# Fillers in two early slots of an attention kernel as rounds of four 32-row TensorE products

## The chip, the cores and the metric

The kernel runs on one core of one Trainium2 chip. The metric is the device time of one execution in microseconds. Before the change three executions took 212.06, 213.21 and 213.5 us; the median is 213.21 us. A fourth execution was profiled.

## The reference: what is computed

Block-sparse attention over 4 batches, 8 heads, 768 positions of 64 values, and then a gated feed-forward layer on its output:

```python
scores = scale * np.matmul(q, k.transpose(0, 1, 3, 2))
...            # mask: neighbouring blocks of 32, first and last block, 3 drawn blocks a row
attn = softmax(np.where(mask, scores, -1000000000.0))
x = (attn @ v) with the heads side by side              # (4, 768, 512)
h = np.maximum(x @ w_in, 0.0);  u, v = the two halves of h
v_n = (v - mean) / sqrt(var + 1e-06)
v_s = np.einsum('ts,bsd->btd', w_spatial, v_n) + b_spatial
out = (u * v_s) @ w_out
```

The mask goes into the scores as extra rows of the contraction: a head's K and Q have 64 rows of data and 24 rows for the blocks, 88 in all. The exponential needs no maximum, since the values are small, and the sum of a row comes from a column of ones next to V.

## The kernel before

All operations are written in one order by hand; each engine runs its own part of that order from the front, and waits on semaphores for what the others make. The middle of the program is a loop over *slots* (line 823). In a slot s the order is: the q·k products of that slot into a tile of two PSUM banks (`qk_unit`, L395 to L412, or `qk_full`, L414), whose exponential ACT then takes into `a_all` (L412, L424); products with V for an earlier slot (`av_unit`, L453, or `av_full`, L471); then whatever was put into the slot with `when`; then pieces of the feed-forward layer from a queue (`product`, L557).

The first slots are the start of the pipeline. Slots 0 to 2 are head 0, slots 3 to 5 head 1, each on two thirds of the queries; slots 6 to 8 are the first third of heads 2 and 3. K and Q arrive by DMA in float32, POOL casts them to bf16 (`nat`, L135), TensorE transposes them into PSUM, and DVE copies them from there into `kq` (L215). Slot 0 transposes the rest of head 0's K (`second`, PSUM tile `ps2`), slot 1 head 1's K and Q (`third`, tile `ps1`, five transposes, then four DVE copies), slot 4 the K and first Q of heads 2 and 3 (`tr_first`, L355). Products with V begin in slot 5, when the first V has been cast.

PSUM has eight banks here: two tiles of two banks each for the q·k products (tag `sc`), two banks with the tag `av`, and the banks `moeA` and `moeB`, which `moe_tag` hands out in turn. A tile whose bank was used before waits until its readers are done.

*Fillers* (L181 to L183) are products of a zero tile `warm` with itself, whose result nobody reads. There are 26 ahead of the first transposes, 6 and 2 among them, and 4 in slot 2 (`FILL3`, line 719). Those four multiply 128 rows by 128 columns into one bank, `moeA`.

Of the kernel before, what the change touches and what calls it, by code (L numbers as in the profile page):

```python
# [10 lines left out]
FP32 = mybir.dt.float32  # L11
# [15 lines left out]
def kernel(  # L27
# [16 lines left out]
    nc = tc.nc  # L44
# [21 lines left out]
    FILL, FILL2, FILL3 = 26, (6, 0, 2), 4  # L66
# [4 lines left out]
    psum = ctx.enter_context(tc.tile_pool(name="psum", bufs=1, space=bass.MemoryType.PSUM))  # L71
# [3 lines left out]
    warm = const.tile([128, 128], BF16)  # L75
# [103 lines left out]
    wps = psum.tile([128, 512], FP32, tag="av", bufs=2)  # L179

    def filler(n, to):  # L181
        for _ in range(n):
            nc.tensor.matmul(out=to[:, 0:128], lhsT=warm, rhs=warm, start=True, stop=True)  # L183

    filler(FILL, wps)

    def ts(out, in0, s1, o0, s2=None, o1=None):
        kw = {} if o1 is None else {"op1": o1}
        nc.vector.tensor_scalar(out=out, in0=in0, scalar1=s1, scalar2=s2, op0=o0, **kw)
# [68 lines left out]
    def moe_tag():  # L258
        moe_tags.rotate(1)
        if moe_tags[0] in held:  # L260
            moe_tags.rotate(1)
        return moe_tags[0]
# [446 lines left out]
    def when(slot, *fns):  # L709
        at.setdefault(slot, []).extend(fns)  # L710

    def c(f, *a, **kw):
        return lambda: f(*a, **kw)
# [2 lines left out]
    ROWS = [(1, 2, 8, qcols(0)), (1, 3, 4, K_), (5, 4, 6, K_), (8, 6, 8, K_), (14, 4, 8, qcols(1, 2))]  # L716
    when(0, second)
    when(1, third)
    when(2, lambda: filler(FILL3, psum.tile([128, 512], FP32, tag=moe_tag(), bufs=1, name="wps")))
    for p, sl in ((1, 4), (2, 7), (3, 10)):  # L720
        when(sl, c(tr_first, p))
    for sl, h0, h1, cs in ROWS:
# [152 lines left out]
```

## Time and profile before

| | |
|---|---|
| profiled execution, time | 213.02 us |
| its span, first to last instruction | 211.1 us |
| time outside the span | 1.9 us |
| PE (matmul) busy | 204.4 us, 97% |
| ACT busy | 170.8 us, 81% |
| DVE busy | 127.2 us, 60% |
| POOL busy | 82.4 us, 39% |
| share of PE in the chain that ended last | 90% |
| granted TensorE clock, mean | 1.000 |

PE is TensorE's matmul side, PEld its weight loads. A matmul's duration in the trace contains its way through the array, so products that follow each other overlap: how fast a stream runs is read from the distance between starts. In the timeline, consecutive instructions of one kind are one row: start, length from the first start to the last end, engine, line, operation, tiles and shapes, count, and in brackets the idle time before it and what ended it. With n products in a row, (length − duration of one) / (n − 1) is the distance of their starts. Durations of one, from the groups by shape in the first 12 us: 0.27 us for 88 x 256, 0.38 for 88 x 512, 0.22 for a transpose of 128 x 128, 0.19 for 128 x 65.

### The profile page before, as it was taken

Reading aid. Unit: us, or ns where it says so; the run is one execution under the profiler, and the core shown is the slowest. Engines: PE = TensorE matmul, PEld = TensorE weight load, DVE = VectorE, ACT = ScalarE, POOL = GpSimd, SP = SyncE. Lnnn points to the kernel's source line nnn. Section 1 sums busy time; section 2 is a strip of 40 time slices with the busy share of each in tenths; the row PEclk is TensorE's granted clock in tenths of the full one; section 3 lists DMA queues with packets and bytes.
Section 4 is the critical chain, followed back from the end, with each engine's and each line's share of the span. In section 5 each row is a group of like instructions: output and inputs, shape, how many; then the busy total and the mean of one; then the engine's idle time right before and its main releaser. Section 6 shows DMA issues by size and latency. Waiting matters only on the chain.

```text
span 211.1 us, 5352 instructions
## 1 busy us (share of the span) xinstructions
PE 204.4 (97%) x2143; PEld 129.6 (61%) x2143; DVE 127.2 (60%) x287; ACT 170.8 (81%) x226; POOL 82.4 (39%) x179
## 2 busy tenths in 40 slices
PE   8799999999999999999999999999999999999992
PEld 6578877756666666665666655665566656544441
DVE  7589786979454533394974454285884433476551
ACT  6988999999999999979998888979989787266021
POOL 5789679877882606062552051151020000012000
PEclk9999999999999999999999999999999999999999
DMA  5999899999999979999981497696101225520265
GB/s 147 335 369 343 240 352 285 271 240 324 264 373 163 308 176 292 210 298 313 189 237 37 109 253 179 215 314 124 37 3 32 55 53 107 198 83 2 50 170 203
DMA packets 63868, 41.96 MB, mean 199 GB/s; under 512 B 45668, under 2 KB 58596, under 8 KB 63844
## 3 DMA queue, kind: packets, MB, share of 16 engines
q1 hardware_dynamic: 63412, 41.24, 74.6%
q10 hardware_dynamic: 432, 0.39, 0.6%
q8 instruction: 16, 0.26, 0.5%
q14 instruction: 8, 0.07, 0.1%
HBM read 24.38 MB, written 6.29 MB: 145 GB/s over the span
## 4 chain that ended last, share of the span: by engine, by line
PE 90%; DMA 3%; DVE 2%; SPq 1%; ACT 1%; POOL 0%; issue 0%; ACTq 0%
PE ps_moe L557 33%; PE ps L420 22%; PE ps_av L471 13%; PE ps_t L557 8%; PE ps L407 6%; PE ps_av L453 4%; PE ps_sc L557 3%; DMA st_v<-in_v_dram 3%; DVE kq L215 1%; SPq L107 1%; PE ps_av L268 1%; PE ps L268 0%; ACT osb L218 0%; DVE xn L436 0%; POOL vv L135 0%
## 5 line engine op out<-in xcount | busy, mean ns | idle before, releaser
L424 ACT ACTIVATE a_all<-ps 128x768 bf16<-128x768 f32 x144 | 113.9, 812 | 14.3 <-PE ps L420 6.4
L420 PE MATMUL ps<-kq 88*128 88x384 bf16 x288 | 70.5, 325 | 0.1
L471 PEld LDWEIGHTS <-a_all 128*128 128x128 bf16 x864 | 46.4, 97 | 20.0
L471 PE MATMUL ps_av<-vv,a_all 128*128 128x65 bf16 x864 | 51.2, 194 | 0.0
L420 PEld LDWEIGHTS <-kq 88*128 88x128 bf16 x288 | 27.9, 98 | 30.5 <-issue 0.9
L557 PE MATMUL ps_moe<-w_in_t,xt 128*128 128x512 bf16 x144 | 44.0, 378 | 0.0
L412 ACT ACTIVATE a_all<-ps 128x1024 bf16<-128x1024 f32 x36 | 35.0, 1025 | 2.0 <-PE ps L407 1.8
L135 POOL CAST nat<-st_k 128x256 bf16<-128x256 f32 (+3 forms) x37 | 16.9, 486 | 42.5 <-DMA st_k<-in_k_dram 42.3
L557 PE MATMUL ps_moe<-vn,w_spt 128*128 128x512 bf16 x108 | 32.7, 378 | 0.0
L435 DVE RECIPROCAL rc<-ps_av 128x6 f32<-128x6 f32 (+1 forms) x36 | 6.7, 186 | 30.7 <-PE ps_av L471 29.2
L594 POOL TENSOR_SCALAR std<-mv 128x3 f32<-128x3 f32 (+1 forms) x9 | 2.1, 238 | 57.1 <-DVE mv L591 43.1
L625 DVE SCALAR_TENSOR_TENSOR un<-ps_moe,b_col,un 128x512 bf16<-128x512 f32 x18 | 13.5, 749 | 16.8 <-PE ps_moe L557 16.2
L407 PE MATMUL ps<-kq 88*128 88x256 bf16 (+1 forms) x140 | 21.6, 275 | 0.9 <-ACT a_all L412 0.7
L557 PE MATMUL ps_moe<-w_out_t,gt 128*128 128x512 bf16 x72 | 21.5, 378 | 0.0
L557 PEld LDWEIGHTS <-xt 128*128 128x128 bf16 x192 | 15.3, 97 | 7.0 <-DVE xt L215 0.2
L436 DVE TENSOR_TENSOR xn<-ps_av,rc 128x384 bf16<-128x384 f32 (+1 forms) x36 | 18.5, 513 | 1.2
L135 POOL CAST vv<-st_v 128x256 bf16<-128x256 f32 (+1 forms) x36 | 17.2, 509 | 3.0 <-DMA st_v<-in_v_dram 2.9
L135 POOL CAST nat<-st_q 128x256 bf16<-128x256 f32 (+1 forms) x38 | 16.3, 458 | 2.6 <-DMA st_q<-in_q_dram 2.4
L590 DVE BATCH_NORM_STATS2 stats<-vn 128x6 f32<-128x512 bf16 x24 | 16.5, 687 | 1.4 <-ACT vn L585 0.9
L407 PEld LDWEIGHTS <-kq 88*128 88x128 bf16 x140 | 12.5, 97 | 4.7 <-issue 0.8
L453 PE MATMUL ps_av<-vv,a_all 128*128 128x65 bf16 x288 | 14.8, 194 | 0.3 <-POOL vv L135 0.3
L453 PEld LDWEIGHTS <-a_all 128*128 128x128 bf16 x288 | 13.7, 98 | 1.8 <-issue 0.6
(84 smaller groups left out, 207.2 us busy)
## 6 DMA issues: line engine op xcount, KB each, us to landing
st_v<-in_v_dram SPq DMA_DIRECT2D x16, 384.0 KB, 5.8
out_dram<-osb SPq DMA_DIRECT2D x23, 256.0 KB, 2.8
st_k<-in_k_dram SPq DMA_DIRECT2D x15, 384.0 KB, 4.6
st_q<-in_q_dram SPq DMA_DIRECT2D x15, 384.0 KB, 5.2
ws_f<-in_moe_w_spatial_dram SPq DMA_DIRECT2D x6, 384.0 KB, 6.4
w_f<-in_moe_w_in_dram SPq DMA_DIRECT2D x8, 256.0 KB, 5.9
w_f<-in_moe_w_out_dram SPq DMA_DIRECT2D x4, 256.0 KB, 4.2
st_q<-in_q_dram SPq DMA_DIRECT2D x2, 128.0 KB, 4.8
```

Source lines behind the costliest of these rows:

```text
L135: eng.tensor_copy(out=dst, in_=src)
L407: nc.tensor.matmul(out=ps[:, at:at + n * TW], lhsT=kq[:, h, ci * 128:(ci + 1) * 128], rhs=kq[:, h, qcols(t0, n)], start=True, stop=True)
L412: nc.scalar.activation(out=out, in_=ps, func=AF.Exp, scale=0.125)
L420: nc.tensor.matmul(out=ps[:, hf * 512:hf * 512 + HALF], lhsT=kq[:, j % H, ci * 128:(ci + 1) * 128], rhs=kq[:, j % H, S + hf * HALF:S + (hf ...
L424: nc.scalar.activation(out=a_ref["h", j][:, ci, :].rearrange("p (b c) -> p b c", b=2), in_=ps.rearrange("p (b c) -> p b c", b=2)[:, :, 0:H ...
L435: nc.vector.reciprocal(out=rc[:, 0:n], in_=ps[:, :, D:VA])
L436: nc.vector.tensor_tensor(out=out, in0=ps[:, :, 0:D], in1=rc[:, 0:n].to_broadcast([128, n, D]), op=ALU.mult)
L453: nc.tensor.matmul(out=av_ref[u][:, to, :], lhsT=a_ref[u][:, at:at + 128], rhs=vv[pp % NVV][:, h, ci, :], start=(ci == 0), stop=(ci == NCH ...
L471: nc.tensor.matmul(out=av_ref[j][:, qc, :], lhsT=a_ref["h", j][:, ci, qc * 128:(qc + 1) * 128], rhs=vv[p % NVV][:, h, ci, :], start=(ci == ...
L557: nc.tensor.matmul(out=ref["ps"][:, 0:w], lhsT=lhs(i), rhs=rhs(i), start=(i == 0), stop=(i == n - 1))
L590: nc.vector.bn_stats(out=stats, in_=self.vn[:, tcc, :])
L625: nc.vector.scalar_tensor_tensor(out=self.un[:, tcc, :], in0=ps, scalar=b_col[:, tcc:tcc + 1], in1=self.un[:, tcc, :], op0=ALU.add, op1=AL ...
```

## The change

The four fillers of slot 2 give way to a new helper, `tiled_filler`, and slot 3 gets one too. The helper takes four PSUM tiles, one in each of the banks `moeA`, `moeB` and the two `av` banks. It issues one product over all 128 rows with 256 columns, then three rounds of four products that each use 32 rows (rows 0 to 31, 32 to 63, 64 to 95, 96 to 127) and one of the four banks, and then one over all rows again. The products of 32 rows have 256 columns in slot 2 and 512 in slot 3. The moving operand reads the 128 columns of `warm` over and over. All that is 14 products where there were 4 in slot 2, and 14 where there were none in slot 3.

```diff
+    def tiled_filler(n):
+        tags = ("moeA", "moeB", "av", "av")
+        to = [psum.tile([128, 512], FP32, tag=x, bufs=2 if x == "av" else 1, name=f"wps{i}")
+              for i, x in enumerate(tags)]
+        rhs = warm.rearrange("p (o n) -> p o n", o=1)
+
+        def mm(i, rs, w):
+            nc.tensor.matmul(out=to[i][:, 0:w], lhsT=warm[rs],
+                             rhs=rhs[rs].to_broadcast([rs.stop - rs.start, w // 128, 128]),
+                             start=True, stop=True)
+
+        mm(0, slice(0, 128), 256)
+        for i in range(3):
+            for r in range(4):
+                mm(r, slice(32 * r, 32 * r + 32), n)
+        mm(0, slice(0, 128), 256)
...
-    when(2, lambda: filler(FILL3, psum.tile([128, 512], FP32, tag=moe_tag(), bufs=1, name="wps")))
+    when(2, c(tiled_filler, 256))
+    when(3, c(tiled_filler, 512))
```

In the built program only TensorE's list differs; DVE, ACT, POOL and SP have the same instructions, in the same order and with the same waits. Three waits on TensorE are new or moved. The second product of 32 rows in slot 2 writes `moeB`, which held `ps1`, so its weight load waits for the last of the four DVE copies of `ps1`. Before, the q·k products of slot 3 waited for the third of these copies and those of slot 4 for the fourth. The first product of slot 3's fillers and the first transpose of slot 4 wait for earlier products on TensorE itself. The call of `moe_tag` for the old fillers is gone, so from slot 4 on `moeA` and `moeB` change places.

## The prediction

> **What bounds the kernel.** I read the table of engines, the chain that ended last, and then the timeline of the first 20 us, where the change lies.
>
> ```profile
> PE 204.4 (97%) x2143; PEld 129.6 (61%) x2143; DVE 127.2 (60%) x287; ACT 170.8 (81%) x226; POOL 82.4 (39%) x179
> ...
> PEclk9999999999999999999999999999999999999999
> ...
> PE 90%; DMA 3%; DVE 2%; SPq 1%; ACT 1%; POOL 0%; issue 0%; ACTq 0%
> ```
>
> TensorE is the chain: 90% of the span. What is not TensorE lies at the start, where loads, casts and DVE copies lead (the chain in order of time has DVE pieces up to 18.05 us, and after that nearly nothing but PE). So the question is how much later TensorE enters its unbroken stretch.
>
> ```profile
> 6.85 1.36 DVE L215 COPY kq<-ps 64x384 bf16<-64x384 bf16 x4 [0.31 <-PE ps L281]
> ...
> 7.08 0.59 PE L407 MATMUL ps<-kq 88*128 88x512 bf16 x2 [0.27 <-ACT a_all L412]
> 7.51 0.39 PE L183 MATMUL wps<-warm 128*128 128x128 bf16 x4
> 8.09 0.60 PE L407 MATMUL ps<-kq 88*128 88x256 bf16 x4 [0.19 <-ACT a_all L412]
> 8.91 0.60 PE L407 MATMUL ps<-kq 88*128 88x256 bf16 x4 [0.23 <-ACT a_all L412]
> 9.35 0.50 PE L268 MATMUL ps<-ident,nat 128*128 128x128 bf16 x6
> 10.34 0.28 PE L268 MATMUL ps<-ident,nat 128*128 128x128 bf16 x2 [0.49 <-POOL nat L135]
> 10.46 0.60 PE L407 MATMUL ps<-kq 88*128 88x512 bf16 x2
> 11.40 0.41 PE L453 MATMUL ps_av<-vv,a_all 128*128 128x65 bf16 x8 [0.34 <-POOL vv L135]
> ...
> 13.24 0.18 DVE L435 RECIPROCAL rc<-ps_av 128x4 f32<-128x4 f32 x1 [0.45 <-PE ps_av L453]
> ...
> 18.10 0.61 PE L407 MATMUL ps<-kq 88*128 88x256 bf16 x4 [0.24 <-DVE kq L215]
> ```
>
> The rows at 7.08, 8.09, 8.91 and 10.46 are the q·k products of slots 2, 3, 4 and 5; the old fillers stand at 7.51, the place of the new ones is after 7.51 and after the row at 8.09. TensorE has idle time there (0.19 + 0.23 + 0.49 + 0.34 us in brackets), and the new fillers may use it. From 18.10 us on the trace has no idle time of TensorE over 0.1 us up to 190 us, so what arrives late there ends late.
>
> **Prices.** Distances of starts, from the rows above: 0.11 us for 256 columns ((0.60 − 0.27)/3), 0.21 for 512 columns, 0.057 for 128 columns, 0.031 for 65 columns ((0.41 − 0.19)/7), which is as fast as the trace shows a weight load with its product to follow another. One product of the trace uses 24 rows (a mask product, between two that use the whole array):
>
> ```profile
> 4.83 0.48 PE L274 MATMUL mq<-kq,bm 88*128 88x256 bf16 x2
> 5.04 0.28 PE L274 MATMUL mq<-kq,bm 24*128 24x256 bf16 x1
> 5.25 0.29 PE L183 MATMUL wps<-warm 128*128 128x128 bf16 x2
> ```
>
> The first of these rows holds the 88-row product at 4.83 and the 24-row one. Each step takes 0.21 us where 256 columns take 0.11: changing over costs 0.10 us, in and again out.
>
> What the trace does not show is four 32-row products beside each other. Per product the bounds are 0.031 us (each starts as soon as its pair can be issued) and 0.11 or 0.21 us (columns one after another), or even 0.21 and 0.31 if each is charged the step of the 24-row row. I take the first: a round's products have their own rows, weights and banks, the program gives none of them a wait on another, and the trace starts independent pairs 0.031 us apart. A round then lasts the longer of 4 × 0.031 = 0.12 and its columns: 0.12 us in slot 2, 0.21 in slot 3. [...]
>
> **The sum, part by part.** Removed: four fillers, 4 × 0.057 = 0.23 us. They stood before an idle time and gain nothing.
>
> Slot 2: full product at 7.51, change-over, first 32-row product at 7.72. The second waits for the fourth DVE copy, which ends at 6.85 + 1.36 = 8.21; a release takes about 0.05 us (the cast of V ends at 11.35, its product starts at 11.40) and a weight load 0.03, so 8.30. Behind this wait stands all of TensorE's list. Then ten more steps of 0.031, 0.11 for the last one's columns, 0.10 to change over, 0.11 for the last full product: slot 3's q·k at 8.93 instead of 8.09, 0.84 late. ACT, which had run without a pause, now waits for it.
>
> Slot 3: 4 × 0.11, then 0.11 + 0.10 to the first 32-row product at 9.58; three rounds to 10.30; 0.10 and 0.11: slot 4's q·k at 10.51 instead of 8.91, 1.60 late.
>
> Slot 4 and 5: the eight transposes now follow at once (the cast they waited for ends at 10.29), which wins back 0.66: slot 5's q·k at 11.40 instead of 10.46, 0.94 late. The exponential of slot 4 starts at 11.15 (fourth product at 10.84, duration 0.27, release 0.04) and that of slot 5 at 12.07, since ACT starts one each 0.92 us; before, 11.09. It ends at 13.09. The DVE copies of the transposes move from 10.66 to 11.61.
>
> Slots 6 and 7: slot 6's q·k needs the first of these copies (12.29) and starts at 12.35, 0.70 late. Slot 7's q·k needs slot 5's PSUM tile, so ACT's end at 13.09: it starts at 13.14 instead of 12.35, 0.79 late. The V products after it release the reciprocal that stood at 13.24, so it comes at 14.03; its 0.45 us of idle time are already used up by the same delay. From the reciprocal on DVE works without a pause until the copy that TensorE awaits at 18.10. So TensorE's unbroken stretch starts 0.8 us later, and so does the end.
>
> 213.02 + 0.8 = **213.8 us** for an execution like the profiled one, which lies 0.2 below the median of the runs shown. POOL and the loads do not wait for this work, and their times stay; the swap of `moeA` and `moeB` I cost at nothing, since both are used alike in turn. Free change-overs would bring 213.4, change-overs of twice the size 214.2.
>
> **Rivals.**
> *The rounds run one after another.* For: the only small-row product of the trace overlaps with nothing. Columns in series make slot 2's fillers 11 × 0.11 after the wait and slot 3's 12 × 0.21: slot 3 at 9.72, slot 4 at 13.1 (4.2 late), slot 5 3.5 late, slot 7 3.4 late, end 216.4. If only the weight loads come one after another (about 0.10 us each by their rows), slot 4 is 2.9 late and the end 215.1. With the 24-row step for every product slot 4 is 6.3 late and the end 218.5.
>
> *The fillers hold a clock that is otherwise lost (the other side).* At the very start products of 128 columns stand 0.107 us apart, and 0.057 from 3.93 on:
>
> ```profile
> 2.76 0.95 PE L183 MATMUL wps<-warm 128*128 128x128 bf16 x7
> ```
>
> If executions other than the profiled one fell back to this half speed between 7.5 and 11.4, for about as long as the start took (0.97 to 3.93), they lose 1.5 us, and holding it ends at 213.0 + 0.8 − 1.5 = 212.3. It decides once fewer than half of the executions hold the speed without the new fillers. Against it: the clock row is full, no spacing of 0.107 comes back, the longest idle time of TensorE is 0.49 us, and the profiled time lies inside the runs. [...]
>
> *The delay is hidden.* If loads of the second and third pair land 0.8 us later than in the trace, DVE's and ACT's work waits for those anyway: 213.0 to 213.2. Against: their casts are done before TensorE asks for them in the new order.
>
> **Chances.** Beside each other 0.68; hidden 0.04; clock held 0.05; loads in series 0.07; columns in series 0.13; a step for each 0.03. The range takes the first case with its bounds and the spread of the runs, the hidden one, and the series cases up to 216.4: 212.9 to 216.4. One per cent, 2.1 us, is about what a measurement can tell from no change: faster 0.02, within 0.79 (the loads-in-series case lies at its edge), slower 0.19.
>
> **What would show it.** The weight load of the second 32-row product waits for DVE until about 8.3; the products of a round start 0.03 us apart; slot 4's q·k starts near 10.5 with no idle time before the transposes; ACT has new pauses before slots 3 and 4; the row now at 18.10 stands near 18.9. I am wrong if the 32-row starts are 0.1 us or more apart, if the row at 18.10 stays in place, or if later stretches change.

## The result, and the profile after

The changed kernel takes 215.0 us (median of 13 runs, 214.46 to 216.31); the kernel before, run beside it, 213.29 us (13 runs, 212.06 to 214.81). The ratio is 1.0089, with a 95% interval of 1.0066 to 1.0113: slower by 0.7 to 1.1%, which is 1.4 to 2.4 us. The forecast was 213.8 us with a range of 212.9 to 216.4. The sign and the range hold; the loss is about twice as large as the sum gave. The profiled execution took 215.0 us and its span is 213.2 us, 2.1 us more than before.

From the page of the changed kernel, the table of engines, the clock row in 40 slices, the DMA queue that carries instructions (packets, MB, share), and the chain by engine:

```profile
PE 204.1 (96%) x2133; PEld 130.0 (61%) x2167; DVE 128.5 (60%) x287; ACT 170.8 (80%) x226; POOL 82.5 (39%) x179
...
PEclk9999999999999999999999999999999999999998
...
q8 instruction: 17, 0.28, 0.5%
...
PE 88%; DMA 5%; DVE 2%; issue 1%; ACT 1%; ACTq 0%; POOL 0%; DVEq 0%
```

There are 24 more weight loads (2167), as the program says; some matmul records are missing. The clock is full up to the last slice. DMA has 5% of the chain instead of 3%, and there are 17 instruction packets where the kernel before has

```profile
q8 instruction: 16, 0.26, 0.5%
```

The timeline of TensorE in the first 20 us of the changed kernel (start, length, engine, line, operation, count, idle time before it and what ended it):

```profile
7.13 0.59 PE L425 MATMUL ps<-kq 88*128 88x512 bf16 x2 [0.16 <-ACT a_all L430]
7.56 0.48 PE L195 MATMUL wps<-warm 128*128 128x256 bf16 x2
8.39 0.72 PE L195 MATMUL wps<-warm 32*128 32x256 bf16 x12 [0.35 <-DVE kq L233]
8.94 0.60 PE L425 MATMUL ps<-kq 88*128 88x256 bf16 x4
9.38 1.25 PE L195 MATMUL wps<-warm 128*128 128x256 bf16 x14
10.46 0.60 PE L425 MATMUL ps<-kq 88*128 88x256 bf16 x4
10.90 0.61 PE L286 MATMUL ps<-ident,nat 128*128 128x128 bf16 x8
11.35 0.60 PE L425 MATMUL ps<-kq 88*128 88x512 bf16 x2
11.79 0.42 PE L471 MATMUL ps_av<-vv,a_all 128*128 128x65 bf16 x8
...
19.29 0.61 PE L425 MATMUL ps<-kq 88*128 88x256 bf16 x4 [0.84 <-DVE kq L233]
```

The fillers stand at 7.56 and 9.38. The second 32-row product waits until 8.39 for DVE, and the transposes at 10.90 follow without idle time. The row that stood at 18.10 is now at 19.29, not near 18.9.

Two narrower windows of the same timeline show the rounds:

```profile
8.39 0.29 PE L195 MATMUL wps<-warm 32*128 32x256 bf16 x4 [0.35 <-DVE kq L233]
...
8.39 0.40 PE L195 MATMUL wps<-warm 32*128 32x256 bf16 x8 [0.35 <-DVE kq L233]
```

One such product lasts 0.27 us (groups by shape). Four take 0.29 from the first start to the last end, so they start together, some 4 ns apart in the single records; eight take 0.11 more, which is one round.

**Where the 2.1 us arise.** I laid ACT's exponentials of both traces beside each other. They are 0.57 to 0.65 us late in slots 6 to 8 (the reciprocal after slot 7 is 0.74 us late, 13.98 instead of 13.24), 1.18 us late from 19 us to about 200 us without change, and the span ends 2.14 us late. So, against this one profile of the kernel before, there are three losses: 0.7 us in the first 14 us, 0.5 us between 14 and 19 us, and 1.0 us in the last 10 us.

*The second loss.* DVE's list from the reciprocal to the row that TensorE awaits, as DVE rows of the two timelines, first the kernel before and then the changed one:

```profile
15.29 0.62 DVE L245 COPY kq<-kq 24x1536 bf16<-24x1536 bf16 x1
```

```profile
13.98 0.18 DVE L453 RECIPROCAL rc<-ps_av 128x4 f32<-128x4 f32 x1 [0.44 <-PE ps_av L471]
...
15.97 1.13 DVE L263 COPY kq<-kq 24x1536 bf16<-24x1536 bf16 x1
```

From the reciprocal to this copy's start it is 2.05 us before (13.24 to 15.29) and 1.99 after. From the copy's end to TensorE's row it is 2.19 us in both (15.91 to 18.10, 17.10 to 19.29). Only the copy itself grew, by 0.51 us. It makes the 24 extra rows of heads 6 and 7 (slot 8 in the list `ROWS`). The POOL rows of the same two stretches, before and after:

```profile
14.68 0.83 POOL L135 CAST nat<-st_k 128x768 bf16<-128x768 f32 x1 [0.20 <-DMA st_k<-in_k_dram]
```

```profile
15.86 0.83 POOL L135 CAST nat<-st_q 128x768 bf16<-128x768 f32 x1 [0.70 <-DMA st_q<-in_q_dram]
```

Before, the copy starts 0.21 us ahead of the end of POOL's cast; after, 0.71 us ahead. It ends some 0.41 us after the cast in both.

*The third loss.* The chain in order of time, changed kernel, near the end (start, length, engine, tile, line):

```profile
200.56 0.76 DVE un L643
201.34 4.38 DMA gt<-un
205.78 1.04 PE ps_sc L575 x4
```

A transposing DMA (`gt<-un`, the gated activations of the last feed-forward part) takes 4.38 us from issue to landing. The same one took 3.14 us before and was on no chain. The table of waits of TensorE from 18 us on names it (who waited for whom, us in all, times, longest), first for the kernel before and then for the changed one:

```profile
PE ps L407 <- DVE kq L215: 0.2, 1, 0.2
```

```profile
PE ps L425 <- DVE kq L233: 0.8, 1, 0.8
PE ps_sc L575 <- DMA gt<-un: 0.8, 1, 0.8
```

In the raw records the 17th packet of instructions, 16 KB, is fetched at 203.32 us, while this DMA runs; the last of the 16 packets of the kernel before is fetched at 182.64. TensorE had begun 117 weight loads at the first fetch and 2139 at the 17th (before: 137 at the first, 2020 at the 16th), so one packet comes about every 126 pairs of weight load and product. That these packets carry TensorE's list I read from this count and from the two programs, which differ in that list alone.

### The profile page after: what moved, and what is told of

Read it like the earlier page. It is cut to its first block, busy times and chain, and to the rows that moved or that the text cites. A ratio compares the mean times of both kernels' runs of the same rounds, so it can differ in the third digit from the quotient of the medians.

```text
span 213.2 us, 5365 instructions
## 1 busy us (share of the span) xinstructions
PE 204.1 (96%) x2133; PEld 130.0 (61%) x2167; DVE 128.5 (60%) x287; ACT 170.8 (80%) x226; POOL 82.5 (39%) x179
## 4 chain that ended last, share of the span: by engine, by line
PE 88%; DMA 5%; DVE 2%; issue 1%; ACT 1%; ACTq 0%; POOL 0%; DVEq 0%
PE ps_moe L575 30%; PE ps L438 22%; PE ps_av L489 12%; PE ps L425 8%; PE ps_t L575 6%; PE ps_av L471 4%; PE ps_sc L575 3%; DMA gt<-un 2%; DMA out_dram<-osb 2%; DMA st_q<-in_q_dram 1%; DVE kq L233 1%; PE ps L286 1%; PE wps L195 1%; PE ps_av L286 1%; ACT osb L236 0%
## 5 line engine op out<-in xcount | busy, mean ns | idle before, releaser
L489 PEld LDWEIGHTS <-a_all 128*128 128x128 bf16 x864 | 46.4, 97 | 20.0
L575 PE MATMUL ps_moe<-w_in_t,xt 128*128 128x512 bf16 x128 | 39.9, 378 | 0.4
L575 PE MATMUL ps_moe<-vn,w_spt 128*128 128x512 bf16 x99 | 30.6, 378 | 0.5
L575 PE MATMUL ps_moe<-w_out_t,gt 128*128 128x512 bf16 x66 | 20.2, 378 | 0.2
L233 DVE COPY kq<-tt 64x1536 bf16<-64x1536 bf16 x24 | 14.4, 599 | 0.3
```

The costliest lines, as they stand in the source:

```text
L233: nc.vector.tensor_copy(out=o, in_=i)
L489: nc.tensor.matmul(out=av_ref[j][:, qc, :], lhsT=a_ref["h", j][:, ci, qc * 128:(qc + 1) * 128], rhs=vv[p % NVV][:, h, ci, :], start=(ci == ...
L575: nc.tensor.matmul(out=ref["ps"][:, 0:w], lhsT=lhs(i), rhs=rhs(i), start=(i == 0), stop=(i == n - 1))
```

## The experiments

Theory A: TensorE's early delay, as in the prediction, is about 0.8 us, and the rest has two causes that were not priced: DVE's copy that meets POOL, and a 17th block of TensorE's instructions that is fetched beside the transposes. Rival B: the products of 32 rows themselves cost something that lasts (a mode, the clock, a bank). Rival C: the wait on the fourth DVE copy makes the loss. In the profiles the loads land up to 0.8 us earlier or later from one execution to the next, so a single profile's early shift is uncertain by some tenths; the medians are better there. The runs were made in four groups, each beside the kernel before (medians 213.21, 212.88, 213.22 and 213.34); the ratios, with 95% intervals in brackets, are to these.

**The changed kernel again (no edit).**

> The changed kernel as it is, once more. Three parts of the loss are read from its first profile: TensorE arrives 0.7 us late at the reciprocal of slot 7, DVE's 24-row copy of slot 8 takes 1.13 instead of 0.62 us because POOL casts meanwhile, and in the last 12 us a transposing DMA of gt lands in 4.4 instead of 3.1 us while a 17th block of 16 KB of TensorE's instructions is fetched. If all three belong to the change: the row at 18.10 before stands near 19.3 again, the list of instruction DMAs has 17 entries with one near 203 us, and TensorE waits some 0.8 us for gt; time 215.0, ratio 1.009. If the second and third are chance of one execution: about 18.9, no wait for gt, and a profiled execution near 214.

215.08 us (7 runs), ratio 1.0082 [1.0050, 1.0114]. The tail is the same: 17 packets, the fetch at 203.35, the DMA lands after 4.38 us, TensorE waits 0.8 us. The copy of slot 8 is not: it took 0.57 us here, since POOL had 0.15 us left when it began, while the loads had put the start later by more. So the tail's loss comes back in each profile, and the copy's depends on where POOL stands.

**Slot 2's fillers alone, and slot 3's alone.**

```diff
-    when(3, c(tiled_filler, 512))
```

> The new fillers in slot 2 alone, none in slot 3 (TensorE has 10 more products than before, not 24). Theory of slack: slot 3's q.k at 8.94 as with the change, slot 4's 0.47 late at 9.38, and the wait for the cast at 10.34 swallows that, so slot 5's stands at 10.46 as before; only ACT stays behind (0.15 us at slot 7): row at 18.10 moves by 0.1 to 0.2 us, time 213.2 to 213.5. Rival, each filler block costs its own length: about half of the loss, +0.85 us.

213.82 us (12 runs), 1.0027 [1.0001, 1.0054]. In the timeline of this kernel slot 3's q·k is 0.65 late, but slot 5's is where it was, at 10.46, up to which the profile of the kernel before had waited for the cast of Q.

```profile
8.74 1.04 PE L425 MATMUL ps<-kq 88*128 88x256 bf16 x8
...
18.17 0.61 PE L425 MATMUL ps<-kq 88*128 88x256 bf16 x4 [0.52 <-DVE kq L233]
```

The unbroken stretch starts 0.07 us late. This kernel has 2153 pairs and fetches a 17th packet too, at 204.42, after the DMA had landed at 203.98; no wait for it, and the end is 0.35 late.

```diff
-    when(2, c(tiled_filler, 256))
+    when(2, lambda: filler(FILL3, psum.tile([128, 512], FP32, tag=moe_tag(), bufs=1, name="wps")))
     when(3, c(tiled_filler, 512))
```

> The four old fillers in slot 2 and the new ones in slot 3 alone (14 more products). Theory of slack: slot 4's q.k at 9.61 instead of 8.91, of which the wait for the cast takes back 0.66, slot 5's at 10.50: row at 18.10 moves by 0.0 to 0.1 us, time as before unless the longer list alone brings a 17th instruction block near the end, which would add up to 0.9. Rival, each block costs its own length: +1.1 us. So with the run before it: near nothing each, and 0.7 together, if it is slack that decides.

213.72 us (12 runs), 1.0015 [0.9989, 1.0042]; 2157 pairs, fetch at 204.46, the DMA landed at 204.43, no wait, 0.08 us lost after the early part. By the medians each half of the change costs 0.5 to 0.6 us, more than expected (the interval of this one still includes no loss), and both together 1.7 to 1.9. Against the profile of the kernel before, slot 2's fillers leave 0.07 us at the unbroken stretch. With slot 3's alone 0.2 to 0.3 us are left in slots 6 to 8 and 0.5 later, but in that profile slot 2 already stands 0.49 us late through its loads and a later cast of Q waits 1.75 us for its load, so what the fillers leave can't be told apart from that. In both profiles the fetch fell just behind the DMA's landing.

**Without the products on rows 32 to 63** (those whose bank the DVE copies must clear; nine products to a block).

```diff
-            for r in range(4):
+            for r in (0, 2, 3):
```

> Both blocks, but without the products on rows 32 to 63, the ones that write the bank that held ps1: nine products of 32 rows in each block, three rounds of three, and no wait for DVE (18 more products than before). If the wait for DVE is most of the early loss: slot 3's q.k at 8.26 instead of 8.94, slot 4's at 9.78 instead of 10.47, slot 5's about 10.67, the row at 18.10 moves by 0.1 to 0.2 us. If it is the fillers' own length: rounds of three last as long as rounds of four, and the row stands near 18.8.

214.68 us (12 runs), 1.0057 [1.0030, 1.0084]. Slot 3's q·k is at 8.35 instead of 8.94 and slot 4's at 9.88 instead of 10.46, so the wait is 0.6 us of the delay there. In slot 6 only 0.06 us of delay is left. Yet the end is 2.16 us late: 0.60 after the copy of slot 8, 0.28 more near 43 us, for which I have no cause, and 1.28 at the end. In this profile POOL's cast of K came late through its load, DVE's copy met it (1.13 us), and the fetch fell beside the DMA once more:

```profile
201.04 4.71 DMA gt<-un
205.80 1.04 PE ps_sc L575 x4
```

Rival C falls: with the wait gone, most of the loss stays, by other ways.

**Short products in the kernel before** (24 of 64 columns, put into TensorE's idle time, so that the list is as long as the changed kernel's, 2167 pairs).

```diff
+    def small_filler(n, to):
+        for _ in range(n):
+            nc.tensor.matmul(out=to[:, 0:64], lhsT=warm, rhs=warm[:, 0:64], start=True, stop=True)
...
+    # eight behind the four fillers of slot 2, eight in slot 3, eight ahead of slot 5
```

> The kernel before with 24 more products, as many as the change adds, but short ones (64 columns, 0.03 us each) on all rows and in places where TensorE waits anyway: 8 behind the old fillers of slot 2, 8 behind slot 3's q.k, 8 ahead of the first V products. Nothing should be late at 18.10 (0.0 to 0.1 us). Theory of the 17th instruction block: it is fetched when the 2138th or so of 2167 weight loads runs, as in the changed kernel, that is near 202.2 us, while the last two transposing DMAs of gt are under way; they land 1 to 1.5 us late, TensorE waits for them, and the end moves by 0.9 to 1.3 us: about 214.3, ratio 1.005. Rival, the late landing comes from the early delay or by chance: no wait for gt, time as before.

214.07 us (9 runs), 1.0048 [1.0026, 1.0070]. No product of 32 rows, no wait on the fourth copy, and still about 1 us slower. Queue table and chain of this kernel:

```profile
q8 instruction: 17, 0.28, 0.5%
```

```profile
198.46 4.68 DMA gt<-un
203.19 1.90 PE ps_t L561 x8
```

The fetch came at 200.69 and hit the first of the last transposing DMAs, which took 4.68 us instead of 3.03. The last 10 us lost 0.61 us. (The early shift of 0.89 us in this profile came from a load that landed late, not from the fillers: slots 6 to 8 are not late, and then a cast of Q waits 1.62 us for its load.) The length of the list alone is a cost.

**The same TensorE time in few wide products** (four and five products over all rows, 2148 pairs).

```diff
-        mm(0, slice(0, 128), 256)
-        for i in range(3):
-            for r in range(4):
-                mm(r, slice(32 * r, 32 * r + 32), n)
-        mm(0, slice(0, 128), 256)
+        every = slice(0, 128)
+        if n == 256:
+            for i, w in ((0, 256), (1, 512), (0, 512), (0, 256)):
+                mm(i, every, w)
+        else:
+            for i in range(5):
+                mm(0, every, 512)
```

> TensorE is held as long as by the new fillers, and waits for the last copy of ps1 in slot 2 too, but with few wide products over all rows: 4 in slot 2 (256, then 512 and 512 and 256 columns) and 5 of 512 in slot 3; 5 products more than before in all, not 24. Theory: the early loss is that of the change (slot 3's q.k near 8.9, slot 4's near 10.4, the row at 18.10 0.7 to 1.2 us late, by whether DVE's copy of slot 8 meets POOL's casts), and the tail is that of before: no fetch while the transposes of gt run, no wait for gt. Time 214.0 to 214.4, some 0.9 us under the changed kernel. Rival, the 32-row products themselves matter (changing over, or what they do to later work): as before the change in the early part, or another early part than this.

215.3 us (6 runs, 213.98 to 217.03), 1.0110 [1.0072, 1.0148]. The expectation missed: five pairs more than the kernel before are enough for a 17th packet. It came at 206.37, where no transposing DMA ran, but the six last output DMAs landed after 2.91 to 4.12 us instead of 2.02 to 2.13, and 0.8 us were lost at the end. Against rival B: full-row products of equal time cost as much as the 32-row ones, within the wide interval.

**Each product over all rows** (no rounds of four: the columns of 24 products one after another).

```diff
-                mm(r, slice(32 * r, 32 * r + 32), n)
+                mm(r, slice(0, 128), n)
```

> The changed kernel, with each of the 24 products of 32 rows as a product over all 128 rows instead (same columns, same banks, same waits, same number of instructions): what the rounds would cost if their products ran one after another. Expected: 12 x 0.11 us in slot 2 and 12 x 0.21 in slot 3, slot 3's q.k near 9.6, slot 4's near 12.8, the row at 18.10 some 3.1 us later than before, and the loss in the tail as with the change if the late block falls on the transposes: 216.5 to 217.5, so 1.5 to 2.4 us over the changed kernel. If the gain of four at a time were an appearance of the trace only: as the changed kernel, 215.0.

217.74 us (5 runs), 1.0217 [1.0190, 1.0244]. The timeline of this kernel:

```profile
8.99 1.48 PE L195 MATMUL wps<-warm 128*128 128x256 bf16 x12 [0.27 <-DVE kq L233]
10.31 0.60 PE L425 MATMUL ps<-kq 88*128 88x256 bf16 x4
10.75 2.97 PE L195 MATMUL wps<-warm 128*128 128x256 bf16 x14
13.56 0.60 PE L425 MATMUL ps<-kq 88*128 88x256 bf16 x4
```

Slot 3's fillers hold TensorE from 10.75 to the q·k at 13.56, 2.81 us, where the rounds of four take 1.08 (9.38 to 10.46). The whole is 2.7 us slower than the changed kernel (217.74 − 215.0). The rounds of four do run beside each other, and this is what the rival of the prediction would have looked like.

**A POOL copy in the kernel before**, to make DVE's copy meet POOL.

```diff
     cast(3, "k", PL)
+    extra = const.tile([KR, 256], BF16, name="extra")
+    nc.gpsimd.tensor_copy(out=extra[MR], in_=hot[MR, 0:2].rearrange("b c p -> b (c p)"))
     cast(3, "q", PL)
```

> The kernel before with one small copy more on POOL (24 x 256, about 0.3 us, into a tile that nobody reads) in the gap between two casts at 15.5 to 15.7 us, where DVE makes its 24-row copy of slot 8. Theory that POOL's work slows such copies: the copy, which took 0.62 us with POOL busy for 0.39 of it, takes 0.8 to 1.1, and the row at 18.10 moves by 0.2 to 0.5 us; time 213.4 to 213.7. Rival, POOL has nothing to do with it: 0.62 us again, no change.

212.84 us (12 runs), 1.0006 [0.9976, 1.0036]: no loss. DVE and POOL rows of this kernel:

```profile
14.99 0.55 DVE L245 COPY kq<-kq 24x1536 bf16<-24x1536 bf16 x1
```

```profile
14.71 0.39 POOL L319 COPY extra<-hot 24x256 bf16<-24x256 bf16 x1
15.17 1.05 POOL L135 CAST nat<-st_q 128x768 bf16<-128x768 f32 x1
```

The expected 0.8 to 1.1 us did not come: the extra copy had only 0.12 us left when DVE began, and DVE's copy took its short time. The cast that POOL began while DVE was copying took 1.05 us instead of 0.83: now POOL waited. So in this profile it was not the overlap that counted, but which of the two began first.

**Fewer pairs with the same change.** The fillers at the very opening (26, 6 and 2 products of 128 columns) are made of products of up to 512 columns, in the changed kernel (2143 pairs, as many as the kernel before) and, as a control, in the kernel before (2116).

```diff
-        for _ in range(n):
-            nc.tensor.matmul(out=to[:, 0:128], lhsT=warm, rhs=warm, start=True, stop=True)
+        left = n * 128
+        src = warm.rearrange("p (o n) -> p o n", o=1)
+        while left:
+            w = min(left, 512)
+            nc.tensor.matmul(out=to[:, 0:w], lhsT=warm,
+                             rhs=src.to_broadcast([128, w // 128, 128]), start=True, stop=True)
+            left -= w
```

> The changed kernel, with the plain fillers of the start written as fewer, wider products: the same 128-column product repeated up to 512 columns, 7 products where there were 26, 2 for 6, 1 for 2. TensorE is kept busy as long as before, but its list has 2143 products again, exactly as many as the kernel before the change. Theory of the 17th instruction block: 16 instruction blocks, no late landing of gt, the end follows the early loss alone: 0.9 us under the changed kernel, 213.8 to 214.3, ratio to before 1.003 to 1.005. Rival, the loss in the tail comes with the early delay or with the 32-row products: 215.0 as the changed kernel.

> The kernel before with the same rewriting of its fillers (those of slot 2 too, one product of 512 columns for four of 128): 2116 products, 27 fewer. It is the control of the run before it: if a shorter list alone helps, or wide opening products change the start, it shows here. Expected: 16 instruction blocks, time as before, 213.0 to 213.4; the difference of the two runs is then the early loss of the change, 0.8 us by the recorded sum, up to 1.2 if DVE's copy of slot 8 usually meets POOL's casts.

Changed kernel: 214.46 us (12 runs), 1.0048 [1.0029, 1.0068]. Control: 213.23 us (12 runs), 0.9993 [0.9976, 1.0011], so the wider opening is worth nothing by itself. The changed kernel with it has 16 packets, the transposing DMA lands after 3.19 us, and the table of waits of TensorE from 16 us on has one line, with none for `gt`:

```profile
q8 instruction: 16, 0.26, 0.5%
```

```profile
PE ps L430 <- DVE kq L238: 0.9, 1, 0.9
```

The shift is 1.4 us from 20 us to the end, without a tail. This splits the loss: 1.23 us (214.46 − 213.23) arise early, and the 17th packet costs the rest, 0.5 us by medians (1.71 − 1.24, each against the kernel before beside it), 0.9 us by ratios ((1.0089 − 1.0048) × 213.29 us; the two intervals just overlap), 0.96 us in the profile. The copy of slot 8 in this profile, and POOL beside it:

```profile
16.12 1.20 DVE L268 COPY kq<-kq 24x1536 bf16<-24x1536 bf16 x1
```

```profile
15.88 1.04 POOL L268 COPY kq<-kq 24x1024 bf16<-24x1024 bf16 x1
```

The early loss has a source that the profile of the kernel before hides. There TensorE waits 0.49 us for the cast of Q, and from slot 2's q·k to slot 5's it takes 3.38 us (7.08 to 10.46). In the kernel with the added POOL copy, which differs from the kernel before only after 14 us, there is no such wait, and it takes 2.80 us:

```profile
7.40 0.59 PE L409 MATMUL ps<-kq 88*128 88x512 bf16 x2 [0.25 <-ACT a_all L414]
...
9.66 0.70 PE L268 MATMUL ps<-ident,nat 128*128 128x128 bf16 x8
10.20 0.60 PE L409 MATMUL ps<-kq 88*128 88x512 bf16 x2
```

It is 2.74 to 2.80 us in all five other profiles without the new fillers, this one among them, and 4.05 to 4.28 us in the three with all of the new ones. So the new fillers hold slot 5 up by 1.3 to 1.5 us where the cast is in time, and by only 0.7 to 0.9 us against the one profile in which it was late.

**The copy made earlier, in the kernel before** (slot 5 instead of slot 8).

```diff
-    ... (5, 4, 6, K_), (8, 6, 8, K_), ...
+    ... (5, 4, 6, K_), (5, 6, 8, K_), ...
```

> The kernel before with DVE's 24-row copy of slot 8 moved to slot 5, behind the one there, into the 0.45 us in which DVE waits ahead of the reciprocal at 13.24. If DVE's list between that reciprocal and the copy that TensorE awaits at 18.10 sets the start of TensorE's unbroken stretch, as the recorded sum holds, the list gets 0.62 us shorter and starts some 0.2 later: the row at 18.10 moves to 17.7 to 17.9, where TensorE itself is the next bound (its idle time there is 0.24 us), and the time falls by 0.2 to 0.4 us, 212.8. If DVE does not set it: no change.

213.08 us (12 runs), 0.9997 [0.9973, 1.0021]. The two copies now stand together and met POOL's casts there (1.18 us each instead of 0.69 and 0.62), and TensorE waited 1.16 us at 15.04 for DVE; the row at 18.08 was then bound by TensorE's own list. The expected gain of 0.2 to 0.4 us did not come, and there was no loss: up to 15 us this kernel has room.

**DVE held up in the kernel before**, by one copy from PSUM that nobody reads.

```diff
         for h in range(2):
             dve_copy(kq[0:D, 2 * p + h, 0:S + TW], ps[h * D:(h + 1) * D, :])
+        if p == 2:
+            dve_copy(spare, ps[0:D, 0:640])
```

> The kernel before with one more DVE copy from PSUM (64 x 640, an estimated 0.48 us between the rows of 64 x 512 at 0.42 and 64 x 1024 at 0.67) ahead of the 24-row copy of slot 8, whose result nobody reads; TensorE's list is not touched (2143 pairs, 16 blocks). If DVE's copies have fixed durations, the 24-row copy starts about 0.5 us later, still takes 0.55 to 0.62 us, the row that stood at 18.10 moves by 0.5 and the median becomes 213.2 + 0.5 = 213.7. If the copy stands still while POOL's instruction runs, it now starts while POOL casts Q (0.83 us, begun at 15.2 to 15.7 in the profiles), with 0.3 to 0.8 us of it left, and takes 0.41 more than what is left, 0.7 to 1.2 us: the row moves by 0.6 to 1.1 and the median becomes 213.8 to 214.3. If the cast of Q comes late through its load and nothing runs on POOL, the copy takes 0.55.

213.84 us (12 runs), 1.0019 [0.9993, 1.0045]. The copy of slot 8 began at 15.49 with 0.21 us of POOL's cast left (the loads were early in this execution) and took 0.62 us: where it meets POOL so late, the delay of 0.5 us passes on as it is, and the median moves by 0.50 us (213.84 − 213.34; the interval includes no change). The case with 0.3 to 0.8 us left did not come about in the profile, so this run does not force the meeting; it only adds a point to the table below.

**The copy's time in the profiles.** POOL's time left is that of the instruction that runs when DVE's copy begins.

| profile | POOL left, us | copy, us |
|---|---|---|
| slot 3 alone; short products; control with wide opening | none | 0.55 |
| POOL copy added | 0.12 | 0.55 |
| changed, again | 0.15 | 0.57 |
| before; DVE held up | 0.21 | 0.62 |
| each product over all rows | 0.34 | 0.75 |
| slot 2 alone | 0.41 | 0.82 |
| changed; without rows 32 to 63 | 0.71, 0.72 | 1.13 |
| few wide products | 0.75 | 1.16 |
| rows early, both copies | 0.78, 0.77 | 1.18 |
| changed with wide opening | 0.79 | 1.20 |

All of them are the larger of 0.55 and the time left plus 0.41 us, within 0.01. The 27 other copies of this shape in the same 14 profiles (three to a profile) keep to it too, up to 1.34 us where 0.92 was left. The copy does its work as if POOL's instruction had to end first. The other side shows in POOL's casts of Q: begun with 0.37, 0.38 and 0.18 us of such a copy left, they took 1.05 us (POOL copy added), 1.07 (control with wide opening) and 0.87 (before) instead of 0.83. What makes the two engines wait for each other, no run shows.

## Why the prediction was half right

*The steps on TensorE up to 14 us were right within 0.06 us.* Predicted, and measured in the first profile of the changed kernel:

| step | predicted, us | measured, us |
|---|---|---|
| slot 3, q·k | 8.93 | 8.94 |
| slot 4, q·k | 10.51 | 10.46 |
| slot 5, q·k | 11.40 | 11.35 |
| slot 6, q·k | 12.35 | 12.29 |
| slot 7, q·k | 13.14 | 13.10 |
| reciprocal | 14.03 | 13.98 |
| TensorE's unbroken stretch | 18.9 | 19.29 |
| end against before | +0.8 | +2.14 (span) |

The wait on the fourth copy, the change-over of 0.10 us (0.206 us from the full product at 7.556 to the 32-row one at 7.762) and the idle time that is won back came as priced. The price of 0.031 us per product of a round was too high: they start 4 ns apart and a round lasts its columns, 0.11 and 0.215 us. In the sum this changed only 0.05 us, since the first wait and the columns ruled. By the distance of rounds four 32-row products of 512 columns take 0.215 us here, as long as one q·k product of 512 columns (0.215 from 7.341 to 7.556).

That the times agree so closely is luck in part. The second profile of the changed kernel has the rows of slots 3 to 7 some 0.64 us later, because slot 2 stands later there (7.94 instead of 7.13). And the 0.66 us that the sum wins back ahead of the transposes come from the late cast in the one profile that it was made from; against the five other profiles without the new fillers there is nothing to win back, and slot 5 is 1.3 to 1.5 us late. That 215.0 lies in the range is luck too: its upper part stood for products in series, which did not come.

*The step that failed first* is "From the reciprocal on DVE works without a pause until the copy that TensorE awaits", from which I concluded that the delay passes through unchanged. It took the copy of 0.62 us as fixed, and it read "POOL and the loads do not wait for this work, and their times stay" as good news. In this profile it makes the second loss: POOL's casts stay where the loads put them, and DVE, 0.7 us later, slides into one. Missing term: 1.13 − 0.62 = 0.51 us. That the copy grows by the law of the table is what 42 copies show together. How often it does so in the changed kernel is not shown: the copy took 1.13 us in one of its profiles and 0.57 in the other, and a run that forces the meeting was not obtained. The medians (1.23 us early loss, 0.49 more than the 0.74 before the copy) can't tell: where the cast is in time, the delay of slot 5 alone is that large.

*The step that was missing altogether* is the end. I wrote that I am wrong "if later stretches change" and priced nothing there, since TensorE has no idle time up to 190 us. But 24 products more are also 24 pairs more in the instruction list, and the kernel before stops just short of needing another packet. Kernels of 2116 and 2143 pairs fetched 16 packets (six kernels), those of 2148 to 2167 fetched 17 (all seven). The price depends on what the fetch meets: 0.1 and 0.3 us where the transposes had landed and one early output DMA was slowed (it landed after 3.14 and 3.61 us instead of 2.02), 0.6 to 1.3 us where it falls beside a transposing DMA or the last output. Missing term: 0.5 to 1.0 us.

*The rivals.* In series: not seen in the changed kernel, and shown by the kernel in which it was made so (217.74). Hidden: no, 1.23 us of early loss stay without the tail. The clock held: the granted clock was full up to the last slice in both kernels (mean 1.000 and 0.997), and every kernel with more fillers was slower or the same, none faster. The free swap of the banks `moeA` and `moeB` left no trace that I could find.

So, between the two profiles, 0.74 + 0.51 + 0.96 us, less the 0.06 us that DVE won back between the reciprocal and the copy (2.05 to 1.99), make the 2.1 us of the profile. The first is the prediction's own sum; two terms are missing.

What stays open: how the early loss of a usual execution divides between the delay of slot 5 and the copy; where between 2143 and 2148 pairs the 17th packet begins (with DVE held up, 2143 pairs, the raw records have one 1.8 us after the last instruction); and why the DMA that runs beside the fetch loses over a microsecond (4.38 us instead of 3.14) to 16 KB. In the records of the changed kernel 28 packets of the transposes that begin 0.46 to 0.79 us after the fetch take 0.97 to 1.29 us instead of some 20 ns, and all end between 205.07 and 205.12, as if one thing held them all. The four other profiles with a fetch beside the last transposes have 18 to 28 such packets there, those without have none; what holds them was not tried.

## What to carry to other kernels

When a stretch moves, don't carry the durations along: check for DVE's copies of this kind which POOL instruction will be running at their new start. Here the copy of 24 x 1536 went from 0.62 to 1.13 us, because POOL's cast, which had waited 0.70 us for its load, still had 0.71 us to go. When instructions are added, count the whole list of that engine and look at the row of the instruction queue and at what runs when the next packet will be fetched: the short products stood in idle time, made slots 6 to 8 no later, and the last 10 us still lost 0.61 us, 190 us behind them. Fewer, wider products avoided the second cost where they left 2143 pairs, and did not at 2148. And look at more than one profile before counting on a wait as slack: the 0.49 us here stood in one of six.

## What I had not expected of the hardware

- A DVE copy of 24 x 1536 bf16 took 0.55 us alone and up to 1.34 beside POOL, in all 42 cases the larger of 0.55 and the POOL instruction's remaining time plus 0.41; three POOL casts of 0.83 us that began during such a copy took 0.87, 1.05 and 1.07.
- Packets of 16 KB in the instruction queue are fetched while the kernel runs, 16 or 17 in the span, one for about 126 pairs of weight load and product; I read them as TensorE's list. In the five profiles with a fetch beside one of the last transposing DMAs, that DMA took 4.38 to 4.71 us, against 3.03 to 3.19 without; with few wide products the last output DMAs, a fetch beside them, took 2.91 to 4.12 instead of 2.02 to 2.13.
- In the changed kernel the four products of 32 rows of a round start within 0.02 us of each other (but for the first of slot 2, which stands ahead of the wait), and a round of 512 columns takes 0.215 us of TensorE, as one product of 88 rows does; changing over cost 0.10 us more, once each way.
